# Normalising and projecting the first query chunk tile by tile, reordering the first loads, and idle matmuls while weights land

## The chip, the cores and the metric

One core of one Trainium2 chip. The metric is the device time of one launch in microseconds (us), the median of several runs. Engines: PE is TensorE, DVE is VectorE, ACT is ScalarE, POOL is GpSimd, SP issues most DMAs.

## The reference, cut to what matters

The program is a conditioned transformer block: a modulation computed from `c`, grouped-query attention with cached keys and values, and a gated MLP. Only the front of the attention is touched.

```python
mod = (silu(c) @ w_mod).reshape(1, 6, 1, -1)              # sa, ca, ga, sb, cb, gb
h = layernorm(x) * (1 + ca) + sa                           # x: 2048 x 512
q = (h @ wq) -> 32 heads of 128                            # 8 groups, 4 query heads each
p = softmax(q k^T / sqrt(128)); o = p v                    # k, v: 8 groups x 2048 x 128
x = x + ga * (o @ wo)
# ... then the second layer norm and the MLP
```

## The kernel before: the parts that the change touches

Queries come in 16 tiles of 128 rows; four tiles are a chunk. A *unit* is one tile with one of the 8 groups, so there are 128 units. A unit has 8 *slots*; a slot computes scores for 256 keys, an exponential on ACT over them, and the value product of the unit before. "Filler" matmuls (query projections, output projections) are put into slots by a table. Functions given to `at(unit, slot, fn)` run ahead of that slot's scores. All of this is a fixed program order on each engine. The code is cut: "..." stands for lines left out.

```python
for i in range(NSLOT):                       # NSLOT = 8
    for fn in later.pop((it, i), []): fn()   # what at() registered
    if it < NU:       qk(it, i)              # 2 score matmuls of 512 columns, then exp on ACT
    if 1 <= it <= NU: pv(it - 1, i)          # 8 value matmuls
    for fn in fill.pop((it, i), []): fn()    # query projection
    if i >= 4 and wf: wf[i - 4]()            # output projection
```

Normalising a chunk has three steps: statistics on the DVE (then the reciprocal root on POOL), normalisation on the DVE, and the *turn*: PE transposes, the DVE copies them out with the modulation. The turn uses two PSUM banks out of a pool of two named `misc`; query projection and output projection use the same pool.

```python
def ln1_turn(j0, n, xns):
    for half in range(2):
        t_ps = bank("misc")          # one of two banks
        ...                          # 2 x n transposes on PE
        ...                          # 2 copies by the DVE into hT, with scale and shift

def ln1_at(it, ch):                  # chunks 1, 2, 3 at units 0, 2, 5
    at(it, 1, lambda: st.update(r=ln1_stats(ch * CT, CT)))
    at(it, 5, lambda: st.update(x=ln1_norm(ch * CT, CT, st["r"])))
    at(it, 7, lambda: ln1_turn(ch * CT, CT, st["x"]))
at(3, 0, mod_rest)                   # the other four parts of the modulation
```

A second, slower path behind a check of the softmax sums stands in the file too; it did not run here.

## Time and profile before

| | before |
|---|---|
| median | 1361.92 us (1361.52 to 1363.76, 3 runs; with one run more, 1361.72) |
| span of the profiled run | 1360.8 us |
| PE busy | 1318.9 us (97%) |
| first score pair of unit 0 | 16.0 us, at half clock |
| first score pair of unit 1 | 27.86 us |
| first score pair of unit 7 | 88.39 us |

The best ruler for this kernel is the start of a unit's first score pair. After unit 7 both orders are the same and PE has no gaps, so the difference at that point is the difference that the end inherits.

### The profile page before, as it was taken

How to read it: one execution, taken by the hardware profiler on the slowest of the kernel's cores; microseconds unless marked ns; L12 is line 12 of the kernel's file. 1: busy time of each engine (PE TensorE's matmuls, PEld its weight loads, DVE VectorE, ACT ScalarE, POOL GpSimd, SP SyncE). 2: the span in 40 equal slices, each digit the busy share in tenths (PEclk: the TensorE clock that was granted, in tenths of full speed). 3: DMA queues.
4: the chain of work that ended last, by engine and by line, in shares of the span. 5: the costliest groups of instructions: out<-in, count | busy, mean ns of one | idle time of the engine just before them, and what ended most of it. 6: DMA issues, size and time to landing. Idle time of an engine off the chain costs nothing.

```text
span 1360.8 us, 27642 instructions
## 1 busy us (share of the span) xinstructions
PE 1318.9 (97%) x12137; PEld 873.7 (64%) x12345; DVE 476.7 (35%) x1171; ACT 1079.6 (79%) x1059; POOL 45.5 (3%) x88
## 2 busy tenths in 40 slices
PE   6999999999999999999999999999999999979997
PEld 4666666666666666666666666666666667634444
DVE  5442222222222222222222222222222566872444
ACT  4789999999999999999999999999999999541000
POOL 1010000000000000000000000000000000110000
PEclk9999999999999999999999999999999999989999
DMA  8120021102211120022010310121111121143200
GB/s 270 28 63 16 13 63 36 21 17 33 62 21 21 32 67 17 16 36 66 17 17 17 83 21 17 18 66 32 21 20 17 25 32 32 25 108 78 67 23 26
DMA packets 141183, 56.53 MB, mean 42 GB/s; under 512 B 131104, under 2 KB 136352, under 8 KB 141056
## 3 DMA queue, kind: packets, MB, share of 16 engines
q1 hardware_dynamic: 137504, 42.17, 14.8%
q0 software_dynamic: 3408, 12.45, 3.6%
q8 instruction: 98, 1.61, 0.5%
q14 instruction: 29, 0.24, 0.1%
q10 hardware_dynamic: 144, 0.07, 0.0%
HBM read 21.63 MB, written 2.10 MB: 17 GB/s over the span
## 4 chain that ended last, share of the span: by engine, by line
PE 93%; DVE 3%; SPq 2%; issue 1%; DMA 1%; POOL 0%; ACT 0%; ACTq 0%; POOLq 0%; DVEq 0%
PE o_ps L901 35%; PE s_ps L879 35%; PE misc L843 7%; PE misc L933 6%; PE misc L1205 6%; PE s_ps L1100 2%; SPq L1012 1%; PE o_ps L1220 1%; PE s_ps L1064 1%; DMA wq_g<-in_A_wq_dram 1%; DVE stz L1081 1%; PE misc L796 0%; PE s_ps L1220 0%; DVE hT L803 0%; DVE z L679 0%
## 5 line engine op out<-in xcount | busy, mean ns | idle before, releaser
L886 ACT ACTIVATE pT<-s_ps 128x1024 bf16<-128x1024 f32 x1024 | 1046.0, 1024 | 106.5 <-PE s_ps L879 30.3
L901 PEld LDWEIGHTS <-pT 128*128 128x128 bf16 x8192 | 559.6, 98 | 241.8
L901 PE MATMUL o_ps<-v,pT 128*128 128x129 bf16 x8192 | 646.3, 220 | 0.0
L879 PE MATMUL s_ps<-qT,kT 128*128 128x512 bf16 x2048 | 609.4, 379 | 10.9 <-DVE qT L852 0.8
L912 DVE RECIPROCAL rall<-o_ps 128x2 f32<-128x2 f32 x256 | 43.6, 170 | 765.3 <-PE o_ps L901 765.2
L879 PEld LDWEIGHTS <-kT 128*128 128x128 bf16 x2048 | 196.7, 97 | 121.2 <-issue 1.5
L843 PE MATMUL misc<-hT,wq_g 128*128 128x512 bf16 (+2 forms) x462 | 169.1, 376 | 0.8 <-DMA wq_g<-in_A_wq_dram 0.8
L933 PE MATMUL misc<-wo_g,oT 128*128 128x512 bf16 x386 | 145.7, 377 | 0.0
L913 DVE TENSOR_TENSOR onorm<-o_ps,rall 128x256 bf16<-128x256 f32 x256 | 108.7, 425 | 8.8
L1205 PE MATMUL misc<-wsp,z 128*128 128x512 bf16 (+2 forms) x555 | 100.5, 336 | 1.9 <-DVE gb L1214 1.4
L852 DVE CAST qT<-misc 128x512 bf16<-128x512 f32 (+1 forms) x129 | 87.3, 676 | 1.7 <-PE misc L843 1.7
L1205 PEld LDWEIGHTS <-z 128*128 128x128 bf16 x560 | 50.6, 98 | 50.4 <-issue 1.9
L946 DVE TENSOR_TENSOR xacc<-misc,xacc 128x512 f32<-128x512 f32 x112 | 76.2, 680 | 0.0
L843 PEld LDWEIGHTS <-wq_g 128*128 128x128 bf16 x528 | 52.2, 100 | 4.0 <-issue 1.5
L933 PEld LDWEIGHTS <-oT 128*128 128x128 bf16 x512 | 50.3, 98 | 0.7
L1214 DVE TENSOR_TENSOR gb<-misc,bsp_bc 128x512 bf16<-128x512 f32 (+2 forms) x35 | 20.4, 584 | 60.9 <-PE misc L1205 60.9
L1100 PE MATMUL s_ps<-hT,win_sb 128*128 128x512 bf16 x109 | 27.2, 408 | 7.3 <-ACT z1T L1108 7.1
L1108 ACT ACTIVATE z1T<-s_ps 128x1024 bf16<-128x1024 f32 x14 | 14.2, 1024 | 20.1 <-PE s_ps L1100 11.6
L1064 PE MATMUL s_ps<-win_sb,hT 128*128 128x448 bf16 x128 | 27.0, 352 | 0.1
L1074 ACT ACTIVATE z<-s_ps 128x896 bf16<-128x896 f32 x16 | 14.7, 917 | 15.0 <-PE s_ps L1064 15.0
L1100 PEld LDWEIGHTS <-win_sb 128*128 128x128 bf16 x112 | 11.6, 103 | 22.5 <-issue 11.0
L712 POOL MEMSET v<- 128x32 bf16 x8 | 1.0, 127 | 715.7 <-issue 615.0
(68 smaller groups left out, 288.8 us busy)
## 6 DMA issues: line engine op xcount, KB each, us to landing
v<-in_A_v_cache_dram POOLq DMA_DIRECT2D x7, 512.0 KB, 6.7
wo_g<-in_A_wo_dram POOLq DMA_DIRECT2D x7, 512.0 KB, 4.8
wq_g<-in_A_wq_dram POOLq DMA_DIRECT2D x7, 512.0 KB, 6.0
wsp<-in_w_mod_dram SPq DMA_DIRECT2D x1, 2048.0 KB, 9.3
oT<-onorm SPq DMA_TRANSPOSE x128, 2.4
out_dram<-yout SPq DMA_DIRECT2D x15, 128.0 KB, 1.7
win_sb<-in_B_w_in_dram SPq DMA_DIRECT2D x1, 1792.0 KB, 13.7
wmod_a<-in_w_mod_dram SPq DMA_DIRECT2D x1, 1024.0 KB, 5.5
```

Source lines behind the costliest of these rows:

```text
L843: nc.tensor.matmul(ps[0][:, o0 : o0 + n], lhsT=wqs[g][:, dt, hh * DH : (hh + 1) * DH], rhs=hTs[ch][:, dt, c0 : c0 + n], start=(dt == 0), s ...
L852: nc.vector.tensor_copy(out=qTs[b][:, hs[0] : hs[-1] + 1, c0 : c0 + n], in_=ps[0][:, 0 : len(hs) * n].rearrange("p (h q) -> p h q", q=n),)
L879: nc.tensor.matmul(s_ps[:, h * 512 : (h + 1) * 512].rearrange("p (r q) -> p r q", r=REP), lhsT=groups[g]["kT"][:, kt * P : (kt + 1) * P], ...
L886: nc.scalar.activation(out=pTs[u][:, 2 * i : 2 * i + 2, :], in_=s_ps[:].rearrange("p (k q) -> p k q", k=2), func=ACT.Exp, scale=inv_sqrt_dh,)
L901: nc.tensor.matmul(o_ps[:, hh % 2, 0 : DH + 1], lhsT=pTs[u][:, kt, hh * P : (hh + 1) * P], rhs=groups[g]["v1"][:, kt, 0 : DH + 1], start=( ...
L912: nc.vector.reciprocal(out=rall[:, c0 : c0 + 2], in_=o_ps[:, :, DH])
L913: nc.vector.tensor_tensor(out=onorms[u][:, hh - 1 : hh + 1, :], in0=o_ps[:, :, 0:DH], in1=rall[:, c0 : c0 + 2].unsqueeze(2).to_broadcast([ ...
L933: nc.tensor.matmul(X_ps[:], lhsT=oTs[u][:, hh, :], rhs=groups[g]["wo"][:, hh, :], start=(hh == 0), stop=(hh == REP - 1),)
L946: nc.vector.tensor_tensor(out=xaccs[j][:], in0=X_ps[:], in1=xaccs[j][:], op=ALU.add)
L1064: nc.tensor.matmul(ps[0][:, hf * 512 : hf * 512 + FC], lhsT=h2Ts[j // CT][:, dt, (j % CT) * P : (j % CT + 1) * P], rhs=win_sb[:, dt, FH + ...
L1100: nc.tensor.matmul(ps[0][:, k * 512 : (k + 1) * 512], lhsT=win_sb[:, dt, f * P : (f + 1) * P], rhs=h2Ts[2 * ch2 + k][:, dt, :], start=(dt ...
L1205: nc.tensor.matmul(g_ps[:, :n], lhsT=z2[:, st, f * P : (f + 1) * P], rhs=wsp[t][:, st, c0 : c0 + n], start=(st == 0), stop=(st == NT - 1),)
```

## The change

Its intent: start the first scores sooner. Query weights are loaded ahead of K; idle matmuls on zeros keep PE busy while the modulation weights land, so that its clock is up; only tile 0 of the first chunk is needed for unit 0, so tiles 1 to 3 are normalised and projected one by one beside units 0 to 2. To make room, statistics, turns and the rest of the modulation move to other slots. The diff is cut; words and pointed brackets stand for code left out.

```diff
@@ loads
-    k_nat = ...; nc.sync.dma_start(k_nat, K of group 0)
-    nc.sync.dma_start(x_sb[:, 1:CT, :])
     load_wq(0, nc.sync)
+    k_nat = ...; for hf in range(2): nc.sync.dma_start(half of k_nat)
+    nc.sync.dma_start(x_sb[:, 1:CT, :])
@@ idle matmuls
+    zeros = late.tile([P, REP, DH], BF16, name="onorm", bufs=3); nc.vector.memset(zeros[:], 0.0)
+    def warm(n):
+        w_ps = bank2()
+        for k in range(n):
+            nc.tensor.matmul(w_ps[:, 0:512]..., lhsT=zeros[:, 0, :], rhs=zeros[:], start=True, stop=True)
+    warm(18)
     mod_columns(0, wmod_a, 0)
+    warm(3)
     ln1_turn(0, 1, xns0)
-    <transposes of K, copies of both halves>
-    rstd0 = ln1_stats(1, CT - 1)
+    warm(4)
     for fn in qproj(0, list(range(REP)), 0, P): fn()
-    xns0 = ln1_norm(1, CT - 1, rstd0)
+    <transposes of K, each half followed by its copy>
@@ table of units
+    for jj in range(1, CT):                                  # tiles 1 to 3 of chunk 0
+        at(jj - 1, 0, statistics of tile jj)
+        at(jj - 1, 1, normalise tile jj)
+        at(jj - 1, 2, turn of tile jj)
+        <16 projection matmuls of 128 columns in slots 4 to 7 of unit jj - 1>
-    at(0, 0, turn of tiles 1 to 3)
-    <their 16 projection matmuls of 384 columns, two per slot of unit 0>
-    at(it, 1, statistics); at(it, 5, normalise); at(it, 7, turn)      # it = 0, 2, 5
+    at(it, 4, statistics); at(it, 7, normalise); at(it + 1, 0, turn)  # it = 0, 2, 5
-    at(3, 0, mod_rest)
+    at(3, 3, mod_rest)
-    <projection of chunk 1: units 1 and 2, one per slot>
+    <the same from unit 1 slot 4 to unit 3 slot 3>
```

More of the change, by code (lines that the diff above doesn't have):

```diff
@@ L697 @@
     nc.sync.dma_start(out=wmod_a[:], in_=wmod_dram[:, :, 0 : 2 * D])
-    k_nat = early.tile([P, SK], BF16, name="kT")
-    nc.sync.dma_start(out=k_nat[:].rearrange("p (t d) -> p t d", d=DH), in_=k_rows[:, 0])
-    nc.sync.dma_start(out=x_sb[:, 1:CT, :], in_=x_dram[:, 1:CT, :])
     groups, wqs, hTs, qTs = {}, {}, {}, {}
@@ L728 @@
     load_wq(0, nc.sync)
+    k_nat = early.tile([P, SK], BF16, name="kT")
+    hk = NKT // 2
+    for hf in range(2):
+        nc.sync.dma_start(
+            out=k_nat[:, hf * SK // 2 : (hf + 1) * SK // 2].rearrange("p (t d) -> p t d", d=DH),
+            in_=k_rows[:, 0, hf * hk : (hf + 1) * hk],
+        )
+    nc.sync.dma_start(out=x_sb[:, 1:CT, :], in_=x_dram[:, 1:CT, :])
     groups[0] = {}
@@ L735 @@
     nc.sync.dma_start(out=win_sb[:], in_=win_dram)
+    zeros = late.tile([P, REP, DH], BF16, name="onorm", bufs=3)
+    nc.vector.memset(zeros[:], 0.0)
+    nc.vector.memset(ones_bf[:], 1.0)
     c_f = res.tile([P, NDT], FP32, name="c_f")
@@ L748 @@
     nc.vector.tensor_copy(out=sc_bf[:], in_=sc[:])
-    nc.vector.memset(ones_bf[:], 1.0)
+    def warm(n):
+        w_ps = bank2()
+        for k in range(n):
+            nc.tensor.matmul(
+                w_ps[:, 0:512].rearrange("p (r d) -> p r d", r=REP), lhsT=zeros[:, 0, :], rhs=zeros[:], start=True, stop=True
+            )
+    warm(18)
     def mod_columns(first, wmod, i0):
@@ L813 @@
     mod_columns(0, wmod_a, 0)
+    warm(3)
     ln1_turn(0, 1, xns0)
-    kT0 = early.tile([P, SK], BF16, name="kT")
-    groups[0]["kT"] = kT0
-    k_ps = bank2()[:].bitcast(BF16)
-    for kt in range(NKT):
-        nc.tensor.transpose(
-            k_ps[:, kt * P : (kt + 1) * P], k_nat[:, kt * P : (kt + 1) * P], ident[:]
-        )
-    for hf in range(2):
-        nc.scalar.copy(
-            out=kT0[:, hf * SK // 2 : (hf + 1) * SK // 2],
-            in_=k_ps[:, hf * SK // 2 : (hf + 1) * SK // 2],
-        )
-    rstd0 = ln1_stats(1, CT - 1)
     def qproj(b, heads, c0, n):
@@ L857, in qproj @@
         return [lambda hh=hh, dt=dt: mm(hh, dt) for hh in heads for dt in range(NDT)]
+    warm(4)
     for fn in qproj(0, list(range(REP)), 0, P):
         fn()
-    xns0 = ln1_norm(1, CT - 1, rstd0)
+    kT0 = early.tile([P, SK], BF16, name="kT")
+    groups[0]["kT"] = kT0
+    k_ps = bank2()[:].bitcast(BF16)
+    for hf in range(2):
+        for kt in range(hf * hk, (hf + 1) * hk):
+            nc.tensor.transpose(
+                k_ps[:, kt * P : (kt + 1) * P], k_nat[:, kt * P : (kt + 1) * P], ident[:]
+            )
+        half = slice(hf * SK // 2, (hf + 1) * SK // 2)
+        nc.scalar.copy(out=kT0[:, half], in_=k_ps[:, half])
     NU = HKV * NT
@@ L1017, with ln1_at @@
     wsp = [None] * NCH
-    def ln1_at(it, ch):
-        st = {}
-        at(it, 1, lambda: st.update(r=ln1_stats(ch * CT, CT)))
-        at(it, 5, lambda: st.update(x=ln1_norm(ch * CT, CT, st["r"])))
-        at(it, 7, lambda: ln1_turn(ch * CT, CT, st["x"]))
-    fill = {}
-    rest0 = qproj(0, list(range(REP)), P, 512 - P)
-    at(0, 0, lambda: ln1_turn(1, CT - 1, xns0))
-    for i in range(NSLOT):
-        fill[0, i] = rest0[2 * i : 2 * i + 2]
-    ln1_at(0, 1)
-    ln1_at(2, 2)
-    ln1_at(5, 3)
-    at(3, 0, mod_rest)
+    fill = {}
+    for jj in range(1, CT):
+        st1 = {}
+        at(jj - 1, 0, lambda jj=jj, st1=st1: st1.update(r=ln1_stats(jj, 1)))
+        at(jj - 1, 1, lambda jj=jj, st1=st1: st1.update(x=ln1_norm(jj, 1, st1["r"])))
+        at(jj - 1, 2, lambda jj=jj, st1=st1: ln1_turn(jj, 1, st1["x"]))
+        rest = qproj(0, list(range(REP)), jj * P, P)
+        for k, fn in enumerate(rest):
+            fill.setdefault((jj - 1, 4 + k // 4), []).append(fn)
+    def ln1_at(it, slot, ch):
+        st = {}
+        at(it, slot, lambda: st.update(r=ln1_stats(ch * CT, CT)))
+        at(it, slot + 3, lambda: st.update(x=ln1_norm(ch * CT, CT, st["r"])))
+        at(it + 1, 0, lambda: ln1_turn(ch * CT, CT, st["x"]))
+    ln1_at(0, 4, 1)
+    ln1_at(2, 4, 2)
+    ln1_at(5, 4, 3)
+    at(3, 3, mod_rest)
     def set_fill(b):
@@ L1038, in set_fill @@
         for k, fn in enumerate(fs):
-            it, slot = ((b - 1) * CT + k // NDT, k % NDT) if b > 1 else (1 + k // 8, k % 8)
+            it, slot = ((b - 1) * CT + k // NDT, k % NDT) if b > 1 else (1 + (k + 4) // 8, (k + 4) % 8)
             fill.setdefault((it, slot), []).append(fn)
```

## The prediction

> **What bounds the kernel now.** I read the page's busy table and chain first, to see which engine sets the end; then the timeline of the first 90 us, since the change touches nothing later; then busy time by stretch.
>
> ```profile
> span 1360.8 us, 27642 instructions
> PE 1318.9 (97%) x12137; PEld 873.7 (64%) x12345; DVE 476.7 (35%) x1171; ACT 1079.6 (79%) x1059; POOL 45.5 (3%) x88
> PE   6999999999999999999999999999999999979997
> ...
> PE 93%; DVE 3%; SPq 2%; issue 1%; DMA 1%; POOL 0%; ACT 0%; ACTq 0%; POOLq 0%; DVEq 0%
> ```
>
> PE is busy 97% of the span and is 93% of the chain that ended last: only the first slice is not full. There are 128 units (one query tile of one key/value group) of 8 slots. A slot without filler is two score matmuls (0.43 us) and eight value matmuls (0.47 us), 0.90 us; one 512-column filler (query or output projection) makes it 1.115 us, and then PE has no gap. A microsecond gained or lost before the steady pattern (about 90 us) therefore moves the end by one microsecond.
>
> ```profile
> core 0: us, PE busy (x) PEld busy (x) DVE busy (x) ACT busy (x) POOL busy (x), PEclk, DMA share, GB/s
> 0.00:7.32 7.32, 0.00 (x0) 0.00 (x0) 2.13 (x9) 1.49 (x2) 1.61 (x10) 1.00 0.64 203
> 7.32:15.91 8.59, 6.62 (x80) 5.59 (x81) 5.63 (x17) 1.93 (x2) 1.12 (x2) 1.00 1.16 334
> 15.91:27.86 11.95, 10.03 (x51) 4.66 (x50) 9.61 (x24) 7.87 (x8) 1.27 (x2) 1.00 1.05 384
> 79.47:150.00 70.53, 69.89 (x684) 48.03 (x695) 19.07 (x49) 64.79 (x64) 0.00 (x0) 1.00 0.12 27
> ```
>
> PE does nothing for 7.32 us, then works sparsely; from 79.47 us on it has no gap. The timeline says why the start is slow:
>
> ```profile
> 11.33 1.89 PE L843 MATMUL misc<-hT,wq_g 128*128 128x128 bf16 x16 [0.79 <-DMA wq_g<-in_A_wq_dram]
> 13.26 0.69 DVE L852 CAST qT<-misc 128x512 bf16<-128x512 f32 x1 [0.99 <-PE misc L843]
> 14.32 1.89 PE L796 MATMUL misc<-ident,xn 128*128 128x128 bf16 x12 [1.10 <-DVE xn L679]
> 16.01 1.06 PE L879 MATMUL s_ps<-qT,kT 128*128 128x512 bf16 x2
> 17.11 1.02 ACT L886 ACTIVATE pT<-s_ps 128x1024 bf16<-128x1024 f32 x1 [4.60 <-PE s_ps L879]
> 20.49 0.71 PE L879 MATMUL s_ps<-qT,kT 128*128 128x512 bf16 x2
> 21.37 0.59 PE L879 MATMUL s_ps<-qT,kT 128*128 128x512 bf16 x2
> 27.86 0.60 PE L879 MATMUL s_ps<-qT,kT 128*128 128x512 bf16 x2 [0.80 <-DVE qT L852]
> ```
>
> The reader is to see three things: the first projection waits for its weights to 11.33 us; a score pair takes 1.06 us until 20.5 us and 0.59 us after (half clock, though the PEclk column says 1.00 throughout); and unit 1 begins at 27.86 us. The third view is how a chunk of four tiles is normalised between units:
>
> ```profile
> 37.92 0.68 DVE L690 BATCH_NORM_STATS2 bnst<-x_sb 128x6 f32<-128x512 bf16 x1
> 42.69 1.38 DVE L679 TENSOR_SCALAR xn<-x_sb,mv,rstd_ln 128x512 bf16<-128x512 bf16 x4 [0.23 <-POOL rstd_ln L675]
> 44.59 0.61 PE L796 MATMUL misc<-ident,xn 128*128 128x128 bf16 x8
> 46.29 0.62 PE L796 MATMUL misc<-ident,xn 128*128 128x128 bf16 x8 [1.09 <-DVE hT L803]
> 46.75 0.59 PE L879 MATMUL s_ps<-qT,kT 128*128 128x512 bf16 x2
> ```
>
> Statistics begin at 37.92, 1.13 us after their slot group began (score pair at 36.79); the last normalised tile is out at 44.07, 7.28 us after it. PE comes for it at 44.59, so it waits only 1.09 us between the halves, for the one free PSUM bank.
>
> **What the Trainium skill says.** "TensorE: Matmul & The Clock Gate", Part 1 (the HAM clock gate): the array starts at half rate, and a free-running window of about 3.4 us of sustained work releases it. The trace agrees on the two rates and shows the switch at 20.5 to 21 us, some 6 us after PE became continuous. The same page's table of specifications calls VectorE's and ScalarE's queues strict first-in first-out. In this trace the DVE runs in program order; that carries the argument below. "DMA: Bandwidth & Descriptors", Specifications, gives about 358 GB/s of HBM per core; the window 7.32 to 15.91 moved 334 GB/s, so the early loads queue for bandwidth and order decides who lands first. No page states how long a rebuilt order takes; that is from the trace.
>
> **The change part by part.** I walked the new order by hand with the durations above.
>
> *Weights before K.* K (512 KB) now queues behind the query weights, which should land near 8.9 instead of 11.3 us (the other way round, K landed at 2.25 + 6.4 = 8.65). K's halves land near 9.5 and 10.2, before PE wants them.
>
> *Idle matmuls.* 18 of 512 columns from 1.1 us: at 0.427 us cold and 0.215 warm, about 9 of each, they end near 7.5 (6.8 to 8.4 by the phase of the clock window), as the modulation weights land (7.3). They sit in time PE had nothing to do. The three after the modulation columns (0.65 us) delay the transposes; the four after that hide behind the DVE.
>
> *Start.* Columns done 8.4; transposes 9.35; four 128-column DVE copies to 10.5 (0.27 each); projection, warm, to 11.4, 1.8 us before 13.2; cast to 12.24. K's transposes 11.4 to 11.9, copy 1.0, then the second half, whose instruction list makes it wait for the first copy: 13.1 to 13.6, second copy to about 14.6. First exponential 14.65 against 17.11. At 0.92 us each (ACT's own pace in unit 0) the eighth ends near 22.1.
>
> *Turn of chunk 1*, now ahead of unit 1: tile 1's copies free the DVE at 16.6; four statistics 3.2, Pool 1.4, four normalisations 1.4, a cast 0.7 give 23.3; the second transposes and then unit 1's scores come at about 23.9. Gain there: 27.86 - 23.9 = **-4.0 us**.
>
> *Work moved later.* Before, tiles 1 to 3 were turned and projected before and during unit 0. Now tile 2 and tile 3 follow in units 1 and 2: 32 matmuls of 128 columns at 0.06 (1.9) and 8 transposes (0.5), in slots PE already fills: **+2.4 us**.
>
> *New waits.* In unit 1, slot 2, PE waits for tile 2's normalisation, which queues on the DVE behind chunk 1's four copies of 0.5: +0.9. At unit 2's start the scores need tile 2's query cast, behind a reciprocal and a multiply: +1.0. In unit 2, slot 2, tile 3's normalisation (0.65 late) and the one-bank wait between its halves (0.8): +1.4. Together **+3.3 us**.
>
> *Chunks 2 and 3.* Statistics now start at slot 4 and the turn comes at slot 0 of the next unit: four slots instead of six. The DVE still needs 7.28 us from slot 4, then 0.55 for the output's reciprocal and multiply and 0.6 to 1.2 for the casts that free the banks. PE arrives after 5.4 us (unit 2, with the small projections) and 4.46 us (unit 5). So unit 3 begins about 9.4 us after slot 4, a wait of 3.1 in place of 1.2 (46.75 - 44.59 less 0.93 of transposes): **+1.9**. Unit 6 begins 9.0 after slot 4; before it was 79.47 - 72.62 = 6.85: **+2.15**.
>
> *Modulation rest*, moved from slot 0 to slot 3 of unit 3, where a query head holds one bank: the second row product waits for the first one's copy (0.7 plus a latency): **+1.0**.
>
> Sum: -4.0 + 2.4 + 3.3 + 1.9 + 2.15 + 1.0 = +6.75 us, after which the order is the old one.
>
> **The rivals.** One: the start is worth more and the waits are hidden, as intended: the chunk turns no longer meet a half-open bank, so both 1.09 us waits go (-2.2), and the start gives -4 to -6. Then about 1357. For it: the 1.09 us waits are real in the trace and each turn now has both banks. Against: the DVE order puts statistics and normalisations ahead of the casts that free those banks. Two: the clock. Unit 0 in the new order is bound by ACT with PE about half busy, and PE then idles 2 us; if the idle matmuls don't release the clock, or it falls back, units 0 to 2 lose another 3 to 5 us: about 1372. Against: from 23.23 to 27.86 the old kernel was also half idle and stayed fast. Three: the loads are the bound, and the weights land no sooner than 10.5: unit 1 begins 1.5 us later, about 1370. Against: they are now third in the queue by size, behind 1.13 MB that was in at 7.3.
>
> **Range and chances.** 1361.9 + 6.75 = 1368.7. My waits are upper readings where a transpose overlaps them, and rival one has perhaps one chance in five, so I put 1367.5, with 1360.5 to 1372.5 for 8 in 10. Two per cent is 27 us; the whole start before unit 1 is only 28, and no wait I can name is of that size: faster 0.01, same 0.985, slower 0.005.
>
> **What would show it.** In the new profile: idle matmuls from about 1 us and a pair of scores at 0.59 us from the first one; the query projection near 10.5 and first exponential near 14.6; unit 1's first scores near 23.9; PE waits for xn and banks of about 3 us at the start of units 3 and 6, against 1.1 before; a second wait inside the modulation rest. If those two turns show PE waiting under 1 us, the DVE argument is wrong and rival one holds; if score pairs of 1.06 us appear after 10 us, rival two does; if the query weights are what the projection waits for, rival three.

## The result, and the profile after

The changed kernel took 1371.83 us (1371.03 to 1373.06, 4 runs) against 1361.72 us for the kernel before: ratio 1.0072, 95% interval 1.0055 to 1.009, about 10 us slower. That is within 2% ("same" by that line) but clear of noise. A ratio here is the mean time of one kernel's runs over that of the other's in the same rounds, so it is not quite the ratio of the medians.

The page of the changed kernel, the line of the chain that ended last:

```profile
PE 91%; DVE 4%; SPq 1%; issue 1%; POOL 1%; DMA 1%; ACT 0%; ACTq 0%; POOLq 0%; DVEq 0%
```

PE's share of the chain fell from 93 to 91%, the DVE's rose from 3 to 4% and POOL's from 0 to 1%: the new time is waiting on the normalisation chain.

The start, from the timeline of the changed kernel (start, duration, engine, line, instruction; in brackets the idle time before and what ended it):

```profile
9.67 1.27 PE L846 MATMUL misc<-hT,wq_g 128*128 128x128 bf16 x16
...
12.93 0.59 PE L894 MATMUL s_ps<-qT,kT 128*128 128x512 bf16 x2
...
23.20 0.59 PE L894 MATMUL s_ps<-qT,kT 128*128 128x512 bf16 x2
```

The intent was met: the projection starts at 9.67 us in place of 11.33, the first score pair takes 0.59 us in place of 1.06 and comes at 12.93 in place of 16.0, and unit 1 begins 4.7 us earlier. What followed took it back. These are PE's larger waits in the same timeline, PE alone:

```profile
25.69 0.40 PE L813 MATMUL misc<-ident,xn 128*128 128x128 bf16 x4 [0.52 <-DVE xn L679]
34.13 0.60 PE L894 MATMUL s_ps<-qT,kT 128*128 128x512 bf16 x2 [0.88 <-DVE qT L855]
36.95 0.28 PE L813 MATMUL misc<-ident,xn 128*128 128x128 bf16 x2 [0.64 <-DVE xn L679]
37.93 0.27 PE L813 MATMUL misc<-ident,xn 128*128 128x128 bf16 x2 [0.69 <-DVE hT L820]
49.45 1.87 PE L813 MATMUL misc<-ident,xn 128*128 128x128 bf16 x16 [3.53 <-DVE qT L855]
58.35 1.02 PE L1017 MATMUL misc<-wsp,lhs_bc 128*128 128x512 bf16 x3 [0.78 <-DVE ga_rows L1024]
84.54 0.23 PE L813 MATMUL misc<-ident,xn 128*128 128x128 bf16 x1 [1.97 <-DVE xn L679]
86.88 1.01 PE L813 MATMUL misc<-ident,xn 128*128 128x128 bf16 x8 [0.67 <-DVE xacc L959]
```

Every one of them names the DVE. In the kernel before, the same stretch, from the start of unit 1 on, held two waits of 1.09 us and one of 0.63. The largest wait of the changed kernel, at 49.45 us (the turn of chunk 2), reads as follows in the timeline with all engines:

```profile
41.40 0.68 DVE L690 BATCH_NORM_STATS2 bnst<-x_sb 128x6 f32<-128x512 bf16 x1
...
46.17 2.10 DVE L679 TENSOR_SCALAR xn<-x_sb,mv,rstd_ln 128x512 bf16<-128x512 bf16 x4 [1.49 <-POOL rstd_ln L675]
...
48.72 1.28 DVE L855 CAST qT<-misc 128x512 bf16<-128x512 f32 x2
...
51.11 1.06 PE L894 MATMUL s_ps<-qT,kT 128*128 128x512 bf16 x2
52.88 0.59 PE L894 MATMUL s_ps<-qT,kT 128*128 128x512 bf16 x2
```

The statistics start late because the program puts them late. The four normalisations end at 48.27; only then does the DVE, in program order, come to the casts that free the PSUM banks of the turn. PE had finished its slots at 45.92. And the score pair after the wait takes 1.06 us: PE's clock had fallen. The windows show it in the column PEclk:

```profile
core 0: us, PE busy (x) PEld busy (x) DVE busy (x) ACT busy (x) POOL busy (x), PEclk, DMA share, GB/s
49.45:51.11 1.66, 1.66 (x16) 1.65 (x16) 1.15 (x3) 0.00 (x0) 0.00 (x0) 0.50 1.13 240
86.88:89.70 2.82, 2.82 (x19) 2.11 (x19) 1.85 (x4) 0.86 (x1) 0.00 (x0) 0.50 1.03 342
```

The ruler, start of the first score pair of a slot in both traces (us):

| | before | after | difference |
|---|---|---|---|
| unit 1, slot 0 | 27.86 | 23.20 | -4.66 |
| unit 2, slot 4 | 41.25 | 40.27 | -0.98 |
| unit 3, slot 4 | 54.78 | 60.33 | +5.55 |
| unit 6, slot 0 | 79.47 | 87.68 | +8.21 |
| unit 7, slot 0 | 88.39 | 97.72 | +9.33 |

The last score pair of the attention comes 9.33 us later too (1172.68 against 1163.35), so the ruler holds up to there. The spans of the two profiled runs differ by 8.4, the medians by 10.1: behind the attention PEclk is 0.50 for about 10 us in the trace of before (1195 to 1205) and for about 7 in that of the change (1206 to 1213). The change doesn't touch that part, and why the two differ there is not shown.

### The profile page after: what moved, and what is told of

Same layout as the page of the kernel before. It is cut to its first block, busy times and chain, and to the rows that moved or that the text cites. A ratio compares the mean times of both kernels' runs of the same rounds, so it can differ in the third digit from the quotient of the medians.

```text
span 1369.2 us, 27771 instructions
## 1 busy us (share of the span) xinstructions
PE 1325.5 (97%) x12193; PEld 877.3 (64%) x12402; DVE 478.7 (35%) x1179; ACT 1079.3 (79%) x1059; POOL 47.0 (3%) x92
## 4 chain that ended last, share of the span: by engine, by line
PE 91%; DVE 4%; SPq 1%; issue 1%; POOL 1%; DMA 1%; ACT 0%; ACTq 0%; POOLq 0%; DVEq 0%
PE o_ps L916 35%; PE s_ps L894 34%; PE misc L948 7%; PE misc L846 6%; PE misc L1225 6%; PE s_ps L1120 2%; SPq L1027 1%; PE o_ps L1240 1%; DVE bnst L690 1%; PE s_ps L1084 1%; DVE stz L1101 1%; DVE xn L679 0%; DMA wmod_a<-in_w_mod_dram 0%; PE s_ps L1240 0%; PE misc L813 0%
## 5 line engine op out<-in xcount | busy, mean ns | idle before, releaser
L948 PE MATMUL misc<-wo_g,oT 128*128 128x512 bf16 x444 | 167.5, 377 | 0.0
L846 PE MATMUL misc<-hT,wq_g 128*128 128x512 bf16 (+1 forms) x437 | 146.0, 355 | 0.0
L855 DVE CAST qT<-misc 128x512 bf16<-128x512 f32 x128 | 87.0, 681 | 1.0 <-PE misc L846 1.0
L1120 PEld LDWEIGHTS <-win_sb 128*128 128x128 bf16 x112 | 11.4, 102 | 21.9 <-issue 10.1
```

Of the source, the lines that this page charges most:

```text
L846: nc.tensor.matmul(ps[0][:, o0 : o0 + n], lhsT=wqs[g][:, dt, hh * DH : (hh + 1) * DH], rhs=hTs[ch][:, dt, c0 : c0 + n], start=(dt == 0), s ...
L855: nc.vector.tensor_copy(out=qTs[b][:, hs[0] : hs[-1] + 1, c0 : c0 + n], in_=ps[0][:, 0 : len(hs) * n].rearrange("p (h q) -> p h q", q=n),)
L948: nc.tensor.matmul(X_ps[:], lhsT=oTs[u][:, hh, :], rhs=groups[g]["wo"][:, hh, :], start=(hh == 0), stop=(hh == REP - 1),)
L1120: nc.tensor.matmul(ps[0][:, k * 512 : (k + 1) * 512], lhsT=win_sb[:, dt, f * P : (f + 1) * P], rhs=h2Ts[2 * ch2 + k][:, dt, :], start=(dt ...
```

## The experiments

Theory: PE waits because the late statistics put the DVE's work, and the bank-freeing casts behind it, after the point where PE needs them; on top of that, these waits let the clock fall. Rivals: the waits are only a matter of bank order; the clock costs nothing; parts of the change at the start are themselves harmful.

**Early statistics.** The changed kernel with only the times of chunks 2 and 3 altered:

```diff
-    ln1_at(2, 4, 2)      # statistics (2,4), normalise (2,7), turn (3,0)
-    ln1_at(5, 4, 3)      # statistics (5,4), normalise (5,7), turn (6,0)
+    ln1_at((1, 4), (2, 3), (3, 0), 2)
+    ln1_at((5, 0), (5, 4), (6, 0), 3)
```

> The changed kernel with one thing altered: the statistics and normalisation of chunks 2 and 3 start earlier (chunk 2: statistics at unit 1 slot 4, normalised at unit 2 slot 3; chunk 3: unit 5 slots 0 and 4), while the turns stay at slot 0 of units 3 and 6. If the late DVE work makes the two long PE waits (3.5 and about 4 us in the changed kernel), they shrink to what the bank-freeing casts leave (about 2 and 1.3 us), the clock does not fall after them, and the time comes down by 6 to 8 us, to about 1364 to 1366. If PE waits there for something else (bank order alone), the time stays within 2 us of 1371.8.

Measured: 1364.19 us, ratio to before 1.0016 (0.9999 to 1.0032). The ratio of the change was 1.0072, so this one move gives back 0.0056, or 7.6 us. Its timeline at the two turns:

```profile
47.40 1.20 PE L813 MATMUL misc<-ident,xn 128*128 128x128 bf16 x16 [0.88 <-DVE qT L855]
48.44 0.59 PE L894 MATMUL s_ps<-qT,kT 128*128 128x512 bf16 x2
...
80.58 0.61 PE L813 MATMUL misc<-ident,xn 128*128 128x128 bf16 x8 [0.66 <-DVE xacc L959]
```

The wait of 3.53 us became 0.88, that for `xn` at unit 6 is gone, and the score pair after the turn takes 0.59 us. What is left (0.88 and 0.66) is the bank order: a cast, and at unit 6 a copy, that has to come first. So the late DVE work was the cause, and the bank order alone is the small part. The 7.6 us hold the half clock after the waits too, which is gone with them; the next run takes it apart.

**Clock kept up in the waits.** The changed kernel with 12 matmuls into an unused PSUM tile ahead of the turns of chunks 2 and 3. The DVE order is untouched, so the waits stay.

```diff
+    def keep_clock():
+        w_ps = bank2()
+        for k in range(12):
+            nc.tensor.matmul(w_ps[:, 0:512], lhsT=ident[:], rhs=hTs[0][:, 0, :], start=True, stop=True)
+        if ch > 1:
+            at(it + 1, 0, lambda: keep_clock())
         at(it + 1, 0, lambda: ln1_turn(ch * CT, CT, st["x"]))
```

> The changed kernel with 12 matmuls whose result nobody reads put ahead of the turns of chunks 2 and 3, in PE's waits there; the order of everything else is kept. If part of the loss is the clock that fell to half after those waits (score pair of 1.06 us at 51 and 88 us, transposes at half speed), the waits stay but score pairs are 0.59 us right after them and the time comes down by 2 to 3 us, to about 1369. If the half clock costs nothing of weight, the time is unchanged (within 0.7 us) or up by the added work.

Measured: 1369.12 us, ratio 1.0051 (1.0034 to 1.0068), against 1.0072: 2.9 us less, by adding work (2.7 by the medians). The intervals of the two ratios overlap, but no run does: the slowest took 1369.59, the fastest of the change 1371.03. Its timeline for PE:

```profile
47.10 2.75 PE L1059 MATMUL s_ps<-hT,ident 128*128 128x512 bf16 x12
50.79 1.20 PE L813 MATMUL misc<-ident,xn 128*128 128x128 bf16 x16 [0.94 <-DVE qT L855]
51.83 0.59 PE L894 MATMUL s_ps<-qT,kT 128*128 128x512 bf16 x2
```

PE still gets to the turn about 3.7 us after its slots (47.10 to 50.79), so the wait is not shorter; but the transposes take 1.20 us in place of 1.87 and the scores 0.59 in place of 1.06. The ruler gives the same: from slot 4 of unit 2 to unit 7 it took 54.70 us (41.62 to 96.32) against 57.45 in the change. The half clock after the waits was worth close to 3 us. In this profiled run the clock also fell once after unit 0 (two score pairs of 1.06 us near 24 us), which the run of the change did not show, though the order up to there is the same; the fall depends on the run. PE's longest wait in the 4 us before it was 0.68 us.

**No idle matmuls.** The changed kernel without `warm(18)`, `warm(3)` and `warm(4)`.

> The changed kernel without its 25 idle matmuls. If they are worth their place, score pairs take 1.06 us through unit 0 (ACT paces that unit at 0.92 us, so little is lost there), the projection and K's transposes run at half speed, and unit 1 begins 1 to 3 us later than 23.2; the time goes up by 1 to 3 us. If the three and four matmuls inside the chain cost more than the clock gives, the time goes down by up to 1 us.

Measured: 1373.14 us, ratio 1.0078 (1.0061 to 1.0095), against 1.0072. In the trace unit 1 begins at 25.20 in place of 23.20: 2.0 us. By time it is 1.3 us on medians, 0.8 by the ratios, and the intervals overlap. The idle matmuls are worth one to two microseconds here; they did no harm.

**Kernel before with the idle matmuls alone** (the 18 ahead of the modulation columns).

> The kernel before with only the 18 idle matmuls added, in the same place as in the changed kernel; loads and order as before. If the half clock of the first 20 us cost the old kernel time by itself, the first projection takes 1.2 us in place of 1.9, unit 0 runs at ACT's pace and unit 1 begins near 26 in place of 27.86: faster than before by about 2 us (1359.8). If the loads and the DVE set the start anyway, within 0.7 us of before.

Measured: 1362.89 us, ratio 1.0008 (0.9991 to 1.0025): no gain, so the first expectation missed. The trace has unit 1 at 27.37 in place of 27.86. The first score pair is at full clock and comes at 15.41, only 0.6 us sooner, because the transposes ahead of it wait 1.66 us (1.10 before) for the DVE to normalise tiles 1 to 3. After that wait the clock fell again: the next two pairs take 1.06 us. The first of them:

```profile
16.81 1.06 PE L890 MATMUL s_ps<-qT,kT 128*128 128x512 bf16 x2
```

With the old schedule a faster PE waits longer, and here it did not stay fast; what a full clock all through unit 0 would give is not shown.

**Kernel before with the new load order alone** (query weights, K in halves, then tiles 1 to 3).

> The kernel before with only the load order of the change (query weights, then K in two halves, then the other tiles of the first chunk); its schedule is kept, no idle matmuls. The first projection should come at about 10 in place of 11.33 us, but the old schedule normalises tiles 1 to 3 before the first scores and their loads now land later (about 11 in place of 9.7 us). If the DVE chain of these three tiles sets the first scores, they come later than 16.0, and the time is up by 0.5 to 2 us. If the query weights set the start, as the chain of the old kernel says, unit 1 begins 1 to 1.5 us earlier than 27.86 and the time is down by as much.

Measured: 1363.65 us, ratio 1.0015 (0.9998 to 1.0031): on medians 2 us slower, at the edge of the interval. From its timeline:

```profile
9.61 1.89 PE L826 MATMUL s_ps<-ident,kT 128*128 128x128 bf16 x16 [0.59 <-DMA kT<-in_A_k_cache_dram]
...
15.76 1.86 PE L801 MATMUL misc<-ident,xn 128*128 128x128 bf16 x12 [2.56 <-DVE xn L679]
...
17.41 1.06 PE L884 MATMUL s_ps<-qT,kT 128*128 128x512 bf16 x2
```

The weights land sooner, but in the old PE order K's transposes stand ahead of the projection and now wait for K, so the projection gains nothing. Tiles 1 to 3 arrive later, and for their normalisation PE waits longest (2.56 us), so the first scores come at 17.41 in place of 16.01. I had expected the projection near 10; it started at 11.29.

**Changed kernel with the loads in the old order.**

> The changed kernel with the loads in the old order (K, other tiles, query weights). If the new load order is what lets the projection start at 9.67 us, it now starts near 11.4, K's transposes and the first scores follow 1.7 us later and so does all that comes after: up by 1.0 to 1.7 us on 1371.8, about 1373. If the DVE chain through tile 1 and chunk 1 sets unit 1's start and has slack at its front, the loss is under 0.7 us.

Measured: 1372.72 us, ratio 1.0079 (1.0063 to 1.0096); K still came in two halves. Unit 1 begins at 25.11 in place of 23.20, 1.9 us later, with PE waiting for `wq_g` until 11.78. By time the loss is about 1 us, within the intervals.

**Tile by tile alone:** old load order and no idle matmuls.

> The changed kernel with the loads in the old order and without idle matmuls: only the tile-by-tile part of the change is left. In single steps the idle matmuls were worth about 2.0 us of unit 1's start (25.20 without them against 23.20) and the load order about 1.9 (25.11 with the old one). If the two are separate, unit 1 begins near 27.1 and the time is near 1375; if they overlap (cold projection behind a late load is the same stretch), near 25.5 to 26.5 and 1373 to 1374. Either way the tile-by-tile part alone keeps at most 0.8 to 2.4 us of the start gain against the 27.86 of the kernel before.

Measured: 1375.23 us, ratio 1.0095 (1.0078 to 1.0111). Unit 1 begins at 26.98, 3.8 us later than in the change (2.0 + 1.9 as separate steps), and 0.9 earlier than before. So idle matmuls and load order simply add up, and both need the tile-by-tile schedule: each alone gains nothing in the old one (both together in the old one were not run), and the tile-by-tile schedule gains 0.9 us without them.

**Early statistics, and the rest of the modulation in pieces.** On top of the first experiment:

```diff
-    at(3, 3, mod_rest)
+    at(4, 5, mod_first)                          # columns and left operands
+    at(4, 7, lambda: mod_row(ga_rows, 2))
+    at(5, 6, lambda: mod_row(gb_rows, 5))
```

> The changed kernel with the early statistics of the first experiment and, in addition, the rest of the modulation in three pieces: columns and their left operands at unit 4 slot 5, the two row products at slot 7 and at unit 5 slot 6, so that no piece waits for a bank or for the DVE. In the changed kernel and in the early-statistics run the two waits in it were 0.49 and 0.78 us. If these are real time on the path, 1.0 to 1.5 us less than the early-statistics run, about 1362.9; if they only move a wait to another place, no difference.

Measured: 1361.35 us, ratio 1.0 (0.9983 to 1.0016) against 1.0016 for early statistics alone. Its trace has no wait at these matmuls. Unit 7 begins 1.9 us sooner than in the early-statistics trace, of which 0.3 was there at unit 1 already, so the pieces gave 1.6 us (2.2 by the ratios; 1.0 to 1.5 was expected). The kernel is now level with the one before.

**A version that keeps the start and drops the waits.** Tile 1 as in the change; then (cut, in words)

```diff
+    at(0, 3, statistics of tiles 2 and 3); at(0, 4, normalise both)
+    at(1, 0, turn, half 0); at(1, 1, turn, half 1)          # one bank each
+    <projection of tiles 2 and 3 together, 256 columns, slots 3 to 6 of unit 1>
+    ln1_at((1, 2), (1, 5), (2, 0), (2, 1), 1)   # statistics, normalise, half 0, half 1
+    ln1_at((2, 2), (2, 6), (3, 2), (3, 3), 2)
+    ln1_at((5, 0), (5, 4), (6, 1), (6, 3), 3)
+    <each query head of chunk 1 within one slot: (2,3) (2,5) (2,7) (3,1)>
+    <rest of the modulation in the three pieces above; K's halves in two PSUM banks>
```

> A version meant to keep the change's early start and lose its waits: tile 1 as in the change, tiles 2 and 3 normalised and projected together in unit 1 (256 columns), chunk statistics at least six slots ahead of their turns, each turn's two halves in separate slots so that one free bank is enough, query heads of chunk 1 each within one slot, the rest of the modulation in pieces, K's two transposed halves in two banks. If the waits named in the trace of the changed kernel (0.7 + 0.5 + 0.9 + 1.3 + 3.5 + 1.3 + about 3 us, and the half clock) are what it lost, this gives unit 1 at about 21.5 and about 1357, that is 0.3 to 0.4% below before. If removing them only uncovers others, it stays at or above 1361.

Measured: 1354.87 us (1354.82 to 1355.71, 4 runs), ratio 0.9952 (0.9935 to 0.9969): 6.7 us faster than before on medians, more than the 1357 expected. It changes many things at once, so what each gave is not shown. PE's busy time in one window of each of before, after and this version, from 20 us to the start of unit 7 or past it (window and its length, then busy us of PE, PEld, DVE, ACT, POOL, the granted clock, DMA share, GB/s):

```profile
20.00:88.40 68.40, 63.08 (x626) 42.56 (x635) 33.90 (x87) 53.99 (x54) 6.71 (x10) 1.00 0.33 88
```

```profile
20.00:98.00 78.00, 65.77 (x650) 45.47 (x659) 38.06 (x99) 50.06 (x50) 7.78 (x13) 0.96 0.29 78
```

```profile
20.00:90.00 70.00, 68.90 (x718) 48.53 (x726) 40.37 (x104) 57.17 (x58) 6.72 (x10) 1.00 0.33 90
```

PE stood still for 5.3 us of its window before, 12.2 after the change, and 1.1 in this version, where unit 7 begins at 80.94 against 88.39 before.

## Why the prediction was right or wrong

The direction, the mechanism and the class were right, and the measured 1371.83 lies inside the range, near its upper end (1372.5). The size was short: +5.6 us (1367.5 against 1361.9; 6.75 by the sum, shaded towards a rival), +10 measured. By its own steps:

- *Start, -4.0:* measured -4.66. The projection was put at 10.5 and came at 9.67, since the columns were done at 8.08 in place of 8.4 and the projection began before the last of the four copies ended (10.00); the sum had it wait for all four.
- *Work moved later and new waits in units 1 and 2, +2.4 and +3.3:* the three waits measured 0.52, 0.88 and 0.64 + 0.69 (the sum 2.7), each where it was put. From unit 1 to slot 4 of unit 2 the difference went from -4.66 to -0.98, +3.7. Four projection matmuls of chunk 1 (0.21 each) had moved out of this stretch into unit 3, and 16 small ones (0.06 each) come only after slot 4, so work and waits together are about 5.5 (an estimate from these durations) against 5.7 forecast.
- *Chunk 2, +1.9:* from slot 4 of unit 2 to unit 3 it took 10.84 us, not 9.4. Two terms were off. The four normalisations took 2.10 us in place of 1.38; in this stretch POOL was clearing a buffer and issuing a load (46.08 to 47.55), and the slow normalisations of chunk 3 in both traces (2.25 and 1.63) stand beside POOL work too. The kept traces say more: in all eleven, each tile in the first 100 us was normalised in 0.39 to 0.42 us, except some that ran while POOL was issuing a load (0.5 to 1.1; of the four at 46.17, one took 1.13). In the three runs that moved chunk 2's normalisation away from that issue (early statistics, the pieces, the last version) each tile took 0.40 or 0.41. How the issue slows the DVE is not shown. The other term is the clock.
- *Chunk 3, +2.15:* 9.51 us from slot 4, not 9.0; against 6.85 before, that is +2.66.
- *Modulation rest, +1.0:* 4.11 us (55.10 to 59.21) in place of 3.30 (47.87 to 51.17), +0.8.
- *The step that failed, by size:* "Two: the clock." The rival was named, but placed at units 0 to 2 and set aside because the old kernel had stayed fast when half idle. Its sign, score pairs of 1.06 us after 10 us, came true at units 3 and 6, and that the time is its 1372 is luck. The prediction itself wrote down a wait of 3.1 us at unit 3 and nearly the same at unit 6, and did not ask what the clock does there. The table "Why this matters for your kernels" in the Trainium skill's page "TensorE: Matmul & The Clock Gate" asks for no PE gaps above about 3 us between bursts. The trace agrees at unit 3: after 3.53 us of idleness PEclk is 0.50. It doesn't show 3 us as a safe limit: at unit 6 PEclk is 0.50 after 4.3 us in which PE did eight transposes (82.57 to 86.88) and waited 1.97 us at the longest, and in other runs the clock fell after waits of at most 0.68 us (near 23 us, idle matmuls at the turns), 1.66 (before with idle matmuls) and 2.56 (before with the new load order). What makes it fall is not shown. Its cost at the two turns can be added up by setting the trace beside that of the early statistics: the transposes ahead of unit 3 took 1.66 us in place of 1.04, its first slot 1.77 in place of 1.12, the second half of the turn at unit 6 0.80 in place of 0.45, and unit 6 itself 10.04 in place of 8.92, together 2.7 us. Keeping PE busy there gave 2.9 us back by the ratios. With it the sum reads 6.75 + 2.9 = 9.65, or 1371.4, against the measured 1371.8. The agreement is partly luck: the start was better than its term and chunk 2 worse.
- *Rival one* (waits hidden, 1357) was shaded in with one chance in five and moved the central number 1.2 us the wrong way. The early statistics show what held it back: the bank conflict it counted on was indeed gone, but the DVE behind it was late. *Rival three* (loads) did not happen: the projection did not wait for its weights in the changed kernel, and did with the old load order.

The time that the start gained was given back twice: first as 128-column work and small DVE waits in units 1 and 2, then as turns for which the DVE could not be ready.

## What to carry to other kernels

When work is moved beside a full engine, walk the helper engine's program order as well: a step whose last result is out 7.3 us after its slot (DVE and POOL) needs that much room before its consumer, and whatever frees the consumer's buffers must not stand behind it. The idle stretch of 3.5 us on PE cost more than its length here, because the work after it ran at half clock; look for score pairs of 1.06 us after a wait, whatever its length. Parts of a start-up (loads, clock, schedule) were worth little one by one here; test them together and apart before judging any.

## What the Trainium skill lacked or had wrong

- "TensorE: Matmul & The Clock Gate", Part 4, says that the full clock doesn't engage for transposes. In these runs transposes do run at the higher clock when it is up: 16 in 1.20 us against 1.87, 8 in 0.61 against 1.01 (the profile lists them as MATMUL). Whether they count as work that brings the clock up or keeps it up is not shown. At both turns PEclk was 0.50 for 3.4 us (49.0 to 52.4, and 86.6 to 90.0).
- The same page, "Back-to-back issue gap", gives about 81 ns per matmul of 128 columns and 131 ns of 512 in a stream with weight loads. Here, in a stream with weight loads, a pair of 512 columns advances PE by 0.43 us (215 ns each) and eight of 129 columns by 0.47 us (59 ns each), which is close to the ~216 and ~56 ns that the same passage keeps for isolated matmuls.
- "DMA: Bandwidth & Descriptors", Specifications, gives about 358 GB/s of HBM per core, and the prediction read its 334 GB/s as close to that. The same view of the kernel before has 384 GB/s for the next 12 us (15.91 to 27.86), loads alone, with one core at work.
- No page read here gives the length of a layer-norm step on these engines: 0.80 us per tile of 128 x 512 for statistics, 1.5 us through POOL for the reciprocal root, 1.38 to 2.25 us for four normalisations.
